# Attention, rational MoE and Sinkhorn MoE in one kernel: a reordered prologue, two weight chunks split inside it, and extra identity matmuls

## The chip, the core and the metric

One core of a Trainium2 chip runs one program. The time is the device time of one execution in microseconds (us); a median of three executions stands for the kernel before. TensorE (PE) does the matmuls, VectorE (DVE), ScalarE (ACT) and GpSimd (POOL) the elementwise work, and SyncE (SP) issues most DMAs. Each engine takes its instructions in the order of its own queue.

## The reference

```
B,H,S,D = 4,8,576,64                     # attention, window 32, plain (heads 0-3) or dilated by 4 (heads 4-7)
attn = softmax(mask(q @ k.T / sqrt(D))) @ v
x    = attn.transpose(0,2,1,3).reshape(2304, 512)
h    = x @ w_in                           # 512 x 2048, float64 in HBM
P    = a0 + a1*h + a2*h^2 + a3*h^3
Q    = 1 + |b0|*|h| + |b1|*h^2
x2   = (P / (Q + 1e-6)) @ w_out           # 2048 x 512
gate = 8 rounds of row and column normalisation of exp(x2 @ w_gate - max)
out  = sum_e gate[:, e] * (relu(x2 @ w1[e]) @ w2[e])     # 8 experts, 512 x 1024 x 512
```

## The kernel before, in words

The program has three stages. A **prologue** computes the attention of batch 0. A **rational loop** of 96 steps (6 token blocks of 384 times 16 slices of 128 hidden columns) computes x2, and the attention of batches 1 to 3 is spread over its steps. Then the expert stage runs to the end.

Batch 0 has 12 groups (head pair `pr`, part `jj`) and its work is cut into pieces: 16 `prep` (transposes of q or k on PE, copied out of PSUM by ACT), 12 `qk` (a mask matmul L363, score matmuls L370; then DVE's maximum L388, ACT's three `Exp` L390, DVE's normalisation L394 and L395, POOL's multiply L396), 12 `tr` (transposes L405, copied out by ACT L410) and 12 `av` (L429; then a 16-bit high part by ACT L229 and a low part by DVE L232, in the scale `s_x1`). `s_x1` comes from a scan of the absolute maximum of half of v (`v_load`, `v_scan` L484) and a chain `pow2_scale` that starts at L207 and passes through PE (L180). `att_load` fetches q and k of one head pair, `att_load_v` the windows of v of one group.

`w_in` comes in four chunks of 512 columns. `wi_load` fetches a chunk as 64-bit words, `wi_conv` turns each of its four 128-row parts into float32 (ACT's `Prelu` L492, DVE's L496 and L497) and takes its absolute maximum (ACT L526), `wi_scale` makes its scale and the coefficients of the rational function, and `wi_split` makes the high and low half-precision parts (ACT L229, DVE L232, 128x512). `wo_load` and `wo_split` do the same for the 16 slices of `w_out`, with L492, L496, L497, L607 and POOL's L611. A loop step takes 12 matmuls L634 to L636 (`h1ps`), the rational function on ACT and DVE that begins at ACT's L657, and five steps later (`LAG`) 12 matmuls L694 to L696.

What runs when is decided in two places. The prologue is a list of pieces with extra calls hung on piece numbers (`extra`), and the loop has numbered slots, four to a step (`at`), filled from tables: `WI_S` for the chunks of `w_in`, `WO` for the slices of `w_out`, and rows of calls for the scan of v's second half. After that a scheduler orders each engine's queue by its own timeline, with attention pieces at raised priority. `load` ties a DMA to the last matmul recorded in `gate_mm`, so that it isn't issued earlier. PSUM has eight one-bank tiles in two rotating groups of four.

Of the kernel before, what the change touches and what calls it, by code (L numbers as in the profile page):

```python
# [10 lines left out]
F32 = mybir.dt.float32  # L11
# [16 lines left out]
def kernel(  # L28
# [14 lines left out]
    nc = tc.nc  # L43
# [287 lines left out]
    def att_prep(b, pr, x):  # L331
# [27 lines left out]
    def att_qk(b, pr, jj):  # L359
# [6 lines left out]
        for i in range(3):  # L366
            j = 3 * jj + i
            for h in range(2):
                hd = slice(h * D, (h + 1) * D)
                nc.tensor.matmul(  # L370
                    bt[hd, i * KW:(i + 1) * KW],
                    st["qT"][hd, j * 64:(j + 1) * 64],
                    st["kT"][hd, j * 64:j * 64 + KW],
                    start=False,
                    stop=i == 2,
                )
        sc = bt[:, 0:3 * KW].rearrange("q (i c) -> q i c", i=3)
        i = b * NG + pr * 3 + jj
# [8 lines left out]
        def after():  # L387
            nc.vector.tensor_reduce(out=sx[:, 0, :], in_=sc, axis=AX, op=ALU.max, negate=True)  # L388
            for i in range(3):
                nc.scalar.activation(p[:, i, :], sc[:, i, :], AF.Exp, bias=sx[:, 0, i:i + 1], accum_out=sx[:, 1, i:i + 1])  # L390
            return norm
# [30 lines left out]
    def att_av(b, pr, jj):  # L422
# [4 lines left out]
        for h in range(2):  # L427
            for i in range(3):
# [51 lines left out]
    def v_scan(hf, i):  # L480
        t = vst.pop((hf, i))
        m = vmx[:, 6 * hf + 2 * i:6 * hf + 2 * i + 2]
        for j in range(2):
            nc.vector.tensor_reduce(out=m[:, j:j + 1], in_=t[:, j * NV // 2:(j + 1) * NV // 2], axis=AX, op=ALU.max, apply_absolute_value=True)  # L484
# [4 lines left out]
    def to_f32(src, y, dst):  # L489
        w = src.rearrange("p (n two) -> p n two", two=2)  # L490
        lo, hi = w[:, :, 0], w[:, :, 1]
        nc.scalar.activation(y, hi.bitcast(F32), AF.Prelu, scale=float(2.0**-112), alpha=-float(2.0**32))  # L492
        d = y.bitcast(I32)
# [27 lines left out]
    def wi_conv(c, kk):  # L521
# [10 lines left out]
        junk = st[:, 0:512].bitcast(F32)  # L532
        bits = to_f32(st, x, x)

# [55 lines left out]
    def wo_split(f):  # L590
# [23 lines left out]


    behind = {}

    def pin(eng, i):
        if eng in behind:
            tc.add_manual_dep(i.ins, behind[eng], mybir.DependencyInfo(mybir.DependencyClass.Sync, mybir.DependencyReason.DATA), reason="behind work that others wait for")  # L620

# [3 lines left out]
    def rat_l1(st, half):  # L625
# [6 lines left out]
        for kk in (2 * half, 2 * half + 1):  # L632
# [505 lines left out]
    ATT = ((1, 0, 14), (2, 15, 38), (3, 43, 62))  # L1138
    WO = [f if f < 8 else 11.75 + (f - 8) // 2 * 1.5 + 0.5 * (f % 2) for f in range(NF1)]
    WI_S = (None, 0, 4, 7.5)  # L1140

# [48 lines left out]
    def at(s, fn, *a):  # L1190
        slots[s].append((fn, a))
# [95 lines left out]

    for c in range(1, 4):
        s = int(4 * WI_S[c])
        for kk in range(KD):  # L1290
            at(s + 1 + 2 * kk, wi_conv, c, kk)
            at(s + (12 if c > 1 else 11) + kk, wi_split, c, kk)
        at(s + 10, wi_scale, c)
    for c in (2, 3):
        at(int(4 * WI_S[c]) - (6 if c == 2 else 4), wi_load, c)
    at(4 * 20, lambda: load(wgr, w_gate.rearrange("(k p) e -> p k e", p=P)))
    at(4 * 26 + 1, wg_prep)
    for i in range(3):
# [27 lines left out]
    for kk in range(KD):  # L1326
# [95 lines left out]
```

## Time and profile before

| | us |
|---|---|
| median of 3 executions | 1957.07 (1953.51 to 1958.82) |
| the profiled execution | 1955.98 |
| its span, first to last instruction | 1954.0 |
| mean granted TensorE clock | 0.981 of full speed |
| PE busy | 1875.1 (96%) |
| DVE busy | 1543.8 (79%) |
| ACT busy | 1217.3 (62%) |
| POOL busy | 493.2 (25%) |

The busy shares are averages over stages with different limits. Of the 40 slices of the span that the page shows, PE is at its lowest in the first four, and the granted clock is below nine tenths in the first three alone. The first 48.9 us slice shows PE, DVE, ACT and the DMA engines at 6, 4, 5 and 6 tenths.

### The profile page before, as it was taken

What the parts mean: (1) busy time and instruction counts of PE and PEld (TensorE: products, weight loads), DVE (VectorE), ACT (ScalarE), POOL (GpSimd) and SP (SyncE); (2) the same over time, 40 slices, a digit from 0 to 9 for tenths busy, and PEclk for the clock granted to TensorE, in tenths of its full rate; (3) what the DMA queues carried; (4) which work ended last, traced back from release to release, by engine and by line L of the source; (5) the groups of instructions that cost most, each with busy time, mean ns of one, the idle gap of its engine ahead of it and who ended that gap; (6) DMA issues with size and microseconds to landing.
All of it is one profiled execution on the core that took longest, in us unless ns stands there. A gap on an engine that the chain in (4) does not pass through costs nothing. (4 is left out here: it accounts for less than half of the span.)

```text
span 1954.0 us, 36520 instructions
## 1 busy us (share of the span) xinstructions
PE 1875.1 (96%) x14202; PEld 1410.8 (72%) x14202; DVE 1543.8 (79%) x2516; ACT 1217.3 (62%) x2182; POOL 493.2 (25%) x489
## 2 busy tenths in 40 slices
PE   6688999999999899999999999999999999999998
PEld 5466777777776677777777777777777777777776
DVE  4799769678998999778688778877878787786754
ACT  5788777777776545647556655664656566465652
POOL 1233422222232023015113211411421231141110
PEclk6789999999999999999999999999999999999999
DMA  6744113122212351564454357345435534633323
GB/s 172 214 135 125 32 38 104 34 59 76 92 38 80 124 157 68 190 185 128 94 141 125 56 120 184 69 109 143 103 62 135 155 74 112 165 87 78 86 54 53
DMA packets 208269, 207.92 MB, mean 106 GB/s; under 512 B 78176, under 2 KB 155488, under 8 KB 208096
## 3 DMA queue, kind: packets, MB, share of 16 engines
q1 hardware_dynamic: 191232, 173.09, 29.4%
q0 software_dynamic: 16864, 32.51, 11.2%
q8 instruction: 111, 1.82, 0.4%
q14 instruction: 62, 0.51, 0.1%
HBM read 155.86 MB, written 49.68 MB: 105 GB/s over the span
## 5 line engine op out<-in xcount | busy, mean ns | idle before, releaser
L922 PEld LDWEIGHTS <-roomA 128*128 128x128 f16 x3276 | 318.9, 98 | 182.1 <-issue 14.2
L922 PE MATMUL l1a<-roomA 128*128 128x384 f16 x1872 | 355.8, 326 | 3.3 <-ACT roomV L971 2.5
L922 PE MATMUL l1b<-roomA 128*128 128x384 f16 x1404 | 273.6, 326 | 5.4 <-DVE roomA L973 3.4
L680 POOL TENSOR_TENSOR roomIG<-roomA,roomIG 128x384 fp32r<-128x384 f32 x96 | 118.2, 1242 | 230.6 <-ACT roomIG L679 206.0
L944 POOL TENSOR_TENSOR roomIG<-roomA 128x384 f32<-128x384 f32 x48 | 60.2, 1254 | 456.8 <-ACT roomA L978 344.3
L1022 PE MATMUL yps<-roomA 128*128 128x256 f16 x630 | 169.9, 273 | 2.4 <-DVE roomV L1048 1.5
L1022 PE MATMUL yps<-roomA,roomV 128*128 128x256 f16 x630 | 168.9, 273 | 3.1 <-DVE roomA L1045 3.1
L1023 PE MATMUL yps<-roomA,roomV 128*128 128x256 f16 x630 | 170.5, 273 | 0.8 <-DVE roomA L885 0.8
L1023 PE MATMUL yps<-roomA 128*128 128x256 f16 x630 | 170.9, 273 | 0.0
L1024 PE MATMUL yps<-roomA,roomV 128*128 128x256 f16 x630 | 169.4, 273 | 0.0
L1024 PE MATMUL yps<-roomA 128*128 128x256 f16 x630 | 169.1, 273 | 0.0
L871 POOL TENSOR_TENSOR roomA<-roomA 128x256 f32<-128x256 f32 x140 | 133.2, 971 | 35.0 <-DVE roomA L885 23.1
L695 PE MATMUL o1ps<-roomIG,roomV 128*128 128x384 f32 x384 | 137.0, 357 | 1.5 <-POOL roomIG L680 1.2
L885 DVE SCALAR_TENSOR_TENSOR roomA<-roomA,sm 128x768 f16<-128x768 f32 (+1 forms) x92 | 112.2, 1232 | 25.1 <-ACT roomA L882 24.3
L634 PE MATMUL h1ps<-roomA 128*128 128x384 f16 x384 | 128.5, 335 | 2.7 <-DVE roomA L660 1.3
L696 PE MATMUL o1ps<-roomIG,roomV 128*128 128x384 f32 x384 | 130.0, 341 | 0.0
L636 PE MATMUL h1ps<-roomA 128*128 128x384 f16 x384 | 127.9, 333 | 0.2 <-DVE roomA L232 0.2
L635 PE MATMUL h1ps<-roomA 128*128 128x384 f16 x384 | 128.0, 333 | 0.0
L944 POOL TENSOR_TENSOR roomIG<-roomV 128x384 f32<-128x384 f32 x48 | 51.1, 1064 | 288.7 <-ACT roomV L978 246.7
L1022 PEld LDWEIGHTS <-roomA 128*128 128x128 f16 x1008 | 98.4, 98 | 28.7 <-DVE roomA L1048 3.4
L1023 PEld LDWEIGHTS <-roomV 128*128 128x128 f16 x1008 | 98.4, 98 | 27.4 <-issue 4.2
L882 ACT ACTIVATE roomA<-roomA,sm 128x768 f16<-128x768 f32 (+1 forms) x92 | 93.9, 1036 | 38.9 <-POOL roomA L871 17.0
(221 smaller groups left out, 4925.5 us busy)
## 6 DMA issues: line engine op xcount, KB each, us to landing
roomA<-xd SPq DMA_DIRECT2D x119, 384.0 KB
roomA<-in_moe_w_dram SPq DMA_DIRECT2D x240, 128.0 KB
roomA<-in_moe_w_dram SPq DMA_DIRECT2D x120, 256.0 KB
out_dram<-roomV POOLq DMA_DIRECT2D x31, 512.0 KB, 5.7
out_dram<-roomA POOLq DMA_DIRECT2D x31, 512.0 KB, 5.8
roomV<-in_moe_w_in_dram SPq DMA_DIRECT2D x16, 512.0 KB
roomA<-in_moe_w_out_dram SPq DMA_DIRECT2D x16, 512.0 KB
xd<-roomA SPq DMA_DIRECT2D x14, 384.0 KB
```

The costliest lines, as they stand in the source:

```text
L634: mm = nc.tensor.matmul(hp, whi, xb[:, 0, kk, :], start=kk == 0, stop=False)
L635: nc.tensor.matmul(hp, whi, xb[:, 1, kk, :], start=False, stop=False)
L636: nc.tensor.matmul(hp, wlo, xb[:, 0, kk, :], start=False, stop=kk == KD - 1)
L680: nc.gpsimd.tensor_tensor(out=gl, in0=g, in1=gh.bitcast(F32), op=ALU.subtract)
L695: nc.tensor.matmul(ob[dd], hi, d["gl"], start=False, stop=False)
L696: nc.tensor.matmul(ob[dd], lo, d["gh"], start=False, stop=last)
L871: pin("p" if pool else "v", eng.tensor_tensor(out=d[:, o, :], in0=a, in1=b, op=ALU.add if w == 0 and n == 0 else ALU.subtract))
L885: pin("v", nc.vector.scalar_tensor_tensor(out=l, in0=x, scalar=sc, in1=h, op0=ALU.mult, op1=ALU.subtract))
L922: mm = nc.tensor.matmul(ps, w[:, wx_, wh, kk * P:(kk + 1) * P], x[:, xh, kk, :], start=start and kk == 0 and wh == 0 and xh == 0, stop=sto ...
L1022: nc.tensor.matmul(o, hh[:, a - 1, c], w[:, m, 0, :], start=i == 0 and half == 0, stop=False)
L1023: nc.tensor.matmul(o, hh[:, a - 1, c], w[:, m, 1, :], start=False, stop=False)
L1024: nc.tensor.matmul(o, hl[:, a - 1, c], w[:, m, 0, :], start=False, stop=i == NP - 1 and (last or half == 1 or b == 3))
```

## The change

1. SP's queue is given q and k of head pair 2 ahead of v's scan, the coefficients `ra` and `rb` after v's first windows, then chunk 0 of `w_in`, then pair 3. Chunk 1 of `w_in` is requested at piece 20 in place of piece 30.
2. Chunks 0 and 1 of `w_in` are converted, scaled and split at fixed pieces (26 and 36 onward). Before, chunk 0 was split in the last pieces, and the calls for chunk 1 stood in steps 0 to 3 of the loop.
3. After each `prep`, `qk` and `av` piece of batch 0, four matmuls of the identity, read as 16-bit words, write 224 otherwise unused columns of the same PSUM tile (`keep_busy`).
4. `pin` orders an instruction behind a recorded one: the `Prelu` of chunks 0 and 1 behind the last `Exp` recorded, that of chunks 2 and 3 and of `w_out`, and the scan of v's second half, behind a step's first `h1ps` matmul.
5. In the loop, chunks 2 and 3 move to steps 2 and 6 (from 4 and 7.5), the second scan from step 1 to step 6, and slices 8 to 15 of `w_out` are spread evenly.

```diff
+    ident_w = ident.bitcast(BF16)
+    def keep_busy(bt, b, c, count):
+        if b < 1:
+            for _ in range(count):
+                nc.tensor.matmul(bt[:, c:c + 224], ident_w[:, 0:P], ident_w[:, 0:224], start=True, stop=True)
...
         for c in range(n):
             nc.tensor.transpose(bt[:, c * w:(c + 1) * w], src[:, n * y + c, :], ident[:w, :w])
+        keep_busy(bt, b, HS, 4)
...
+        keep_busy(bt, b, 3 * KW, 4)
         sc = bt[:, 0:3 * KW].rearrange("q (i c) -> q i c", i=3)
...
-                nc.scalar.activation(p[:, i, :], sc[:, i, :], AF.Exp, bias=sx[:, 0, i:i + 1], accum_out=sx[:, 1, i:i + 1])
+                e = nc.scalar.activation(p[:, i, :], sc[:, i, :], AF.Exp, bias=sx[:, 0, i:i + 1], accum_out=sx[:, 1, i:i + 1])
+            behind["x"] = e.ins.name
...
+        keep_busy(bt, b, 288, 4)
...
+            if hf:
+                pin("m", r)
...
-        nc.scalar.activation(y, hi.bitcast(F32), AF.Prelu, scale=float(2.0**-112), alpha=-float(2.0**32))
+        i = nc.scalar.activation(y, hi.bitcast(F32), AF.Prelu, scale=float(2.0**-112), alpha=-float(2.0**32))
+        pin(late, i)
...
-        bits = to_f32(st, x, x)
+        bits = to_f32(st, x, x, "x" if c < 2 else "m")
...
-            bits = to_f32(x, y, y)
+            bits = to_f32(x, y, y, "m")
...
                 gate_mm[0] = mm.ins
+                behind["m"] = mm.ins.name
...
-    WO = [f if f < 8 else 11.75 + (f - 8) // 2 * 1.5 + 0.5 * (f % 2) for f in range(NF1)]
-    WI_S = (None, 0, 4, 7.5)
+    WO = [f if f < 8 else f + 2.25 for f in range(NF1)]
+    WI_S = (None, None, 2, 6)
...
-    at(4 * 13, coefs, 1, 0, 4)
+        at(4 * 6 + 8 * i, v_load, 1, i, "x2_4")
+        at(4 * (6 + 2) + 8 * i, v_scan, 1, i)
+    at(4 * 13, v_scale, 1)
+    at(4 * 14 + 2, coefs, 1, 0, 4)
...
     att_load(0, 1, "R1")
+    att_load(0, 2, "R2")
+    for i in range(3):
+        v_load(0, i, f"x2_{3 + i}")
+    for i in range(2, 4):
+        att_load_v(i)
     nc.sync.dma_start(out=abt[:, 0:4], in_=ra.partition_broadcast(P))
     nc.sync.dma_start(out=abt[:, 4:6], in_=rb.partition_broadcast(P))
-    for i in range(3):
-        v_load(0, i, f"x2_{3 + i}")
-    att_load(0, 2, "R2")
-    for i in range(2, 4):
-        att_load_v(i)
+    wi_load(0)
+    att_load(0, 3, "R3")
     for i in range(4, 8):
         att_load_v(i)
-    att_load(0, 3, "R3")
...
-    extra[12].append(lambda: wi_load(0))
-    extra[30].append(lambda: wi_load(1))
+    extra[20].append(lambda: wi_load(1))
...
-        extra[30 + 2 * kk].append(lambda kk=kk: wi_conv(0, kk))
-        extra[n - 4 + kk].append(lambda kk=kk: wi_split(0, kk))
-    extra[n - 4 - 1].append(lambda: wi_scale(0))
+    for c, x in ((0, 26), (1, 36)):
+        for kk in range(KD):
+            extra[x + kk].append(lambda c=c, kk=kk: wi_conv(c, kk))
+            extra[x + 8 + kk].append(lambda c=c, kk=kk: wi_split(c, kk))
+        extra[x + 7].append(lambda c=c: wi_scale(c))
```

On SP, from the second head pair's q and k onward, the queue of the kernel before holds these rows (`in_v_dram` with 128x1536 is v's scan, `abt` the coefficients; L166 is `load`):

```order
L280 DMA roomA<-in_q_dram 96x6x64 x2
L280 DMA roomA<-in_k_dram 96x6x64 x2
L1309 DMA abt<-in_moe_a_dram 128x4
L1310 DMA abt<-in_moe_b_dram 128x2
L166 DMA roomA<-in_v_dram 128x1536 x3
L280 DMA roomA<-in_q_dram 72x8x64 x2
L280 DMA roomA<-in_k_dram 72x8x64 x2
L304 DMA roomA<-in_v_dram 96x3x64 x2
```

From the same point the changed kernel's queue holds these:

```order
L293 DMA roomA<-in_q_dram 96x6x64 x2
L293 DMA roomA<-in_k_dram 96x6x64 x2
L293 DMA roomA<-in_q_dram 72x8x64 x2
L293 DMA roomA<-in_k_dram 72x8x64 x2
L166 DMA roomA<-in_v_dram 128x1536 x3
L317 DMA roomA<-in_v_dram 96x3x64 x2
L315 DMA roomA<-in_v_dram 64x2x64
L317 DMA roomA<-in_v_dram 96x2x64 x2
L1328 DMA abt<-in_moe_a_dram 128x4
L1329 DMA abt<-in_moe_b_dram 128x2
L166 DMA roomV_136<-in_moe_w_in_dram 128x1024 x2
L166 DMA roomV_139<-in_moe_w_in_dram 128x1024 x2
```

Between v's scan and chunk 0 of `w_in` there are now five loads of v's windows and the two of the coefficients; before there were four for pair 2, 17 for v and four for pair 3. Pair 3's four and 17 for v come next, and then chunk 1; before, 18 for v stood between chunk 0 and chunk 1.

On ACT, around the first `Prelu` of chunk 0 (L492; `p` and `roomA,sx` are exponentials, `avps` parts of x), the kernel before has:

```order
L390 ACTIVATE p,sx<-scps,sx 128x96 x6
L229 ACTIVATE roomA<-avps,sm 128x192
L492 ACTIVATE roomV_268<-roomV_268 128x512
L390 ACTIVATE roomA,sx<-scps,sx 128x96 x3
L229 ACTIVATE roomA<-avps,sm 128x192
L492 ACTIVATE roomV_268<-roomV_268 128x512
```

The changed kernel has, around its first `Prelu` of chunk 0 (L511) and up to that of chunk 1 (which reads `roomV_255`):

```order
L405 ACTIVATE roomA,sx<-scps,sx 128x96
L511 ACTIVATE roomV_136<-roomV_136 128x512 x2
L405 ACTIVATE roomA,sx<-scps,sx 128x96 x2
L235 ACTIVATE roomA<-avps,sm 128x192
L369 ACTIVATE roomV_255<-qkps 128x288 x2
L511 ACTIVATE roomV_136<-roomV_139 128x512 x2
L369 ACTIVATE roomV_255<-qkps 128x288
L546 ACTIVATE roomV_136,sm<-roomV_136 128x512
...
L405 ACTIVATE roomA,sx<-scps,sx 128x96 x3
L235 ACTIVATE roomA<-avps,sm 128x192
L511 ACTIVATE roomV_139<-roomV_255 128x512 x2
```

The conversions stay among the exponentials and copies of batch 0, with the `Prelu`s in pairs.

On PE, the first score matmuls of head pair 1 (`scps<-roomV`) stood in one run in the kernel before:

```order
L405 MATMUL ptps<-ident,p 96x128 x3
L363 LDWEIGHTS ident_b
L363 MATMUL scps<-masks,ident_b 128x288
L370 MATMUL scps<-roomV_221 64x96 x18
L429 MATMUL avps<-roomA 64x64 x6
```

In the changed kernel each six of the eighteen are followed by four pairs of weight load and matmul on the identity (the first pair is shown, and then the next av):

```order
L421 MATMUL ptps<-ident,p 96x128 x3
L377 LDWEIGHTS ident_b
L377 MATMUL scps<-masks,ident_b 128x288
L384 MATMUL scps<-roomV_255 64x96 x6
L254 LDWEIGHTS ident
L254 MATMUL scps<-ident 128x224
...
L445 MATMUL avps<-roomA 64x64 x6
```

The program adds 160 such pairs, four for each of the 40 pieces.

## Rows read from the trace of the kernel before

**Rows 1.** Busy time by stretch: five engines, PE clock, DMA share, GB/s.
```profile
0.00:26.00 26.00, 17.19 (x139) 14.13 (x139) 12.54 (x43) 12.71 (x52) 6.44 (x24) 0.80 0.67 184
26.00:71.00 45.00, 27.76 (x258) 21.12 (x257) 24.32 (x71) 29.50 (x101) 4.76 (x9) 0.61 0.61 174
76.00:140.00 64.00, 52.70 (x392) 37.13 (x390) 61.27 (x123) 55.90 (x150) 23.44 (x22) 0.92 0.61 188
140.00:200.00 60.00, 52.68 (x399) 38.85 (x399) 55.06 (x115) 48.84 (x125) 22.44 (x21) 0.91 0.40 110
200.00:300.00 100.00, 100.00 (x763) 78.76 (x762) 72.58 (x132) 75.06 (x189) 33.18 (x37) 1.00 0.16 41
```

**Rows 2.** ACT's waits from 0 to 76 us: total, times, longest.
```profile
ACT roomV L492 <- DMA roomV<-in_moe_w_in_dram: 11.9, 2, 7.3
ACT roomA L390 <- DVE sx L388: 6.5, 4, 3.4
ACT roomA L355 <- PE qkps L347: 5.2, 3, 3.1
```

**Rows 3.** Timeline of ACT: start, duration, instruction, idle before and its cause.
```profile
25.22 0.41 ACT L229 ACTIVATE roomA<-avps,sm 128x192 f16<-128x192 f32 x1
40.64 0.66 ACT L492 ACTIVATE roomV<-roomV 128x512 f32<-128x512 f32 x1 [7.27 <-DMA roomV<-in_moe_w_in_dram]
54.90 0.66 ACT L492 ACTIVATE roomV<-roomV 128x512 f32<-128x512 f32 x1 [4.63 <-DMA roomV<-in_moe_w_in_dram]
75.18 0.67 ACT L657 ACTIVATE roomA<-h1ps,cf 128x384 f32<-128x384 f32 x1
215.58 0.67 ACT L657 ACTIVATE roomA<-h1ps,cf 128x384 f32<-128x384 f32 x1 [0.35 <-PE h1ps L636]
```

**Rows 4.** Timeline of SP's queue in the prologue.
```profile
34.39 3.13 SPq L166 DMA_DIRECT2D roomV<-in_moe_w_in_dram  x4
37.63 12.99 SPq L315 DMA_DIRECT2D roomA<-in_v_dram  x18
50.69 1.85 SPq L166 DMA_DIRECT2D roomV<-in_moe_w_in_dram  x4
```

**Rows 5.** ACT by line and form, 0 to 220 us: busy us, mean ns.
```profile
L229 ACT ACTIVATE roomA<-roomV,sm 128x512 f16<-128x512 f32 x16 | 10.3, 728 | 1.4 <-DVE sm L225 1.4
L355 ACT ACTIVATE roomA<-qkps 128x288 f32<-128x288 f32 x32 | 13.3, 431 | 5.4 <-PE qkps L347 5.2
```

**Rows 6.** Busy time by stretch, two shorter ones.
```profile
14.00:16.00 2.00, 0.00 (x0) 0.09 (x1) 0.89 (x6) 1.08 (x7) 0.67 (x1) 0.85 1.00 418
20.00:30.00 10.00, 8.96 (x65) 7.04 (x65) 5.31 (x20) 6.80 (x27) 2.15 (x4) 0.50 0.49 105
```

**Rows 7.** Timeline of PE, third pair's transposes, av matmuls, first loop step.
```profile
36.83 1.19 PE L347 MATMUL qkps<-ident,roomA 72*128 72x72 f32 x8 [2.36 <-issue]
...
26.92 1.18 PE L429 MATMUL avps<-roomA 96*64 96x64 f32 x12
...
33.28 0.73 PE L429 MATMUL avps<-roomA 96*64 96x64 f32 x12
...
72.60 0.53 PE L634 MATMUL h1ps<-roomA 128*128 128x384 f16 x1
72.92 0.53 PE L635 MATMUL h1ps<-roomA 128*128 128x384 f16 x1
...
73.50 0.33 PE L634 MATMUL h1ps<-roomA 128*128 128x384 f16 x1
73.66 0.33 PE L635 MATMUL h1ps<-roomA 128*128 128x384 f16 x1
```

**Rows 8.** Timeline of DVE, the wait for the coefficients.
```profile
14.24 0.21 DVE L559 TENSOR_SCALAR sm<-abt 128x1 int32<-128x1 int32 x2 [2.22 <-DMA abt<-in_moe_b_dram]
```

**Rows 9.** ACT's waits from 76 to 218 us.
```profile
ACT roomA L657 <- PE h1ps L636: 3.7, 4, 2.2
```

More of the change, by code (lines that the diff above doesn't have):

```diff
@@ L198, in across_sum, with pin @@
         nc.vector.tensor_scalar(out=out_, in0=bt[:, 0:n], scalar1=1e-9, scalar2=None, op0=ALU.add)
+    behind = {}
+    def pin(eng, i):
+        if eng in behind:
+            tc.add_manual_dep(i.ins, behind[eng], mybir.DependencyInfo(mybir.DependencyClass.Sync, mybir.DependencyReason.DATA), reason="behind work that others wait for")
     def delayed(fn, k):
@@ L483, in v_scan, with to_f32 @@
         for j in range(2):
-            nc.vector.tensor_reduce(out=m[:, j:j + 1], in_=t[:, j * NV // 2:(j + 1) * NV // 2], axis=AX, op=ALU.max, apply_absolute_value=True)
+            r = nc.vector.tensor_reduce(out=m[:, j:j + 1], in_=t[:, j * NV // 2:(j + 1) * NV // 2], axis=AX, op=ALU.max, apply_absolute_value=True)
+            if hf:
+                pin("m", r)
     def v_scale(hf):
         return pow2_scale(vmx[:, 6 * hf:6 * hf + 6], 6, 14, s_x1[:, hf:hf + 1], i_x1[:, hf:hf + 1], lag=hf)
-    def to_f32(src, y, dst):
+    def to_f32(src, y, dst, late):
         w = src.rearrange("p (n two) -> p n two", two=2)
         lo, hi = w[:, :, 0], w[:, :, 1]
-        nc.scalar.activation(y, hi.bitcast(F32), AF.Prelu, scale=float(2.0**-112), alpha=-float(2.0**32))
+        i = nc.scalar.activation(y, hi.bitcast(F32), AF.Prelu, scale=float(2.0**-112), alpha=-float(2.0**32))
+        pin(late, i)
         d = y.bitcast(I32)
@@ L613, in wo_split @@
         return s1
[L616 to L620, printed above, removed]
     cur = {}
@@ L1286, in run_slot @@
                 at(s + 1, more)
-    for c in range(1, 4):
-        s = int(4 * WI_S[c])
+    for c in (2, 3):
+        s = 4 * WI_S[c]
+        at(s - 6, wi_load, c)
         for kk in range(KD):
             at(s + 1 + 2 * kk, wi_conv, c, kk)
-            at(s + (12 if c > 1 else 11) + kk, wi_split, c, kk)
+            at(s + 12 + kk, wi_split, c, kk)
         at(s + 10, wi_scale, c)
-    for c in (2, 3):
-        at(int(4 * WI_S[c]) - (6 if c == 2 else 4), wi_load, c)
     at(4 * 20, lambda: load(wgr, w_gate.rearrange("(k p) e -> p k e", p=P)))
@@ L1298 @@
     for i in range(3):
-        at(4 * 1 + 8 * i, v_load, 1, i, "x2_4")
-        at(4 * (1 + 2) + 8 * i, v_scan, 1, i)
-    at(4 * (1 + 8), v_scale, 1)
-    at(4 * 13, coefs, 1, 0, 4)
+        at(4 * 6 + 8 * i, v_load, 1, i, "x2_4")
+        at(4 * (6 + 2) + 8 * i, v_scan, 1, i)
+    at(4 * 13, v_scale, 1)
+    at(4 * 14 + 2, coefs, 1, 0, 4)
     att_load(0, 0)
@@ L1325 @@
     n = len(pcs)
-    for kk in range(KD):
-        extra[30 + 2 * kk].append(lambda kk=kk: wi_conv(0, kk))
-        extra[n - 4 + kk].append(lambda kk=kk: wi_split(0, kk))
-    extra[n - 4 - 1].append(lambda: wi_scale(0))
+    for c, x in ((0, 26), (1, 36)):
[3 more added lines that the diff above has]
+        extra[x + 7].append(lambda c=c: wi_scale(c))
     for f in range(2):
```

## Prediction

> **What bounds the kernel now.** I read the busy times by stretch first. From 200 us on PE is busy 100.00 of 100 us at the full clock (2.4 GHz, granted 1.00), so there the time is PE's and nothing that the change moves shortens it [rows 1]. Before that PE isn't the limit. From 76 to 200 us DVE is busy 116.3 of 124 us (61.27 + 55.06) and ACT 104.7, while PE has 18.6 us of idle time: the loop's first steps carry all the conversions and splits of w_in and w_out and wait for DVE and ACT. From 0 to 71 us, the prologue, no engine is the limit by its sum: PE 45.0, DVE 36.9, ACT 42.2 us busy. That is a chain with holes, and PE's clock is 0.80 and 0.61 there, which is much time at 1.2 GHz.
>
> The holes are seen in ACT's waits. The largest is 11.9 us in two waits: the `Prelu` of a chunk of w_in stands in ACT's queue ahead of batch 0's exponentials and waits for its DMA [rows 2], 7.27 us at 40.64 and 4.63 us at 54.90 [rows 3]. ACT is in order, so attention waits behind it. SP's timeline says why: chunk 0 was issued at 34.39, and chunk 1 at 50.69 after 18 small loads that took 12.99 us to issue [rows 4]. The loop's first evacuation (L657) starts at 75.18, that of step 20, where PE has become the limit, at 215.58 [rows 3]. What the change takes from the first, with the work ahead of step 20 unchanged, it takes from the end.
>
> **The waits for w_in.** In the new order chunk 0 follows v's scan and seven small loads. Up to its end SP has asked for 12 loads of 144 KB (pairs 0 to 2), 2.36 MB of scan, about 0.6 MB of v and 2.1 MB of w_in: 6.8 MB. The old queue moved 4.8 MB in 26 us (184 GB/s [rows 1]), and large loads alone ran at 418 GB/s [rows 6]; the remaining 2.0 MB take 5 us, so chunk 0 is there by some 31 us, and ACT, which starts on x at 25.22 [rows 3], comes to its `Prelu` after some 5 us of copies and exponentials, near 31. That wait goes. Chunk 1 then stands behind pair 3 and 17 loads of v. At 12.99/18 = 0.72 us each [rows 4], 21 loads are 15 us; from an issue of chunk 0 that ends near 23 to 25 us it is issued at 38 to 40 and its first part lands 4.2 us later (50.69 to 54.90), at 42 to 44. ACT has by then done about 17 us of work since 25.22 and arrives at 42 to 43. I leave 1 us of wait, with ends of 0 and 5. Term: -11.9 + 1 = -10.9 us.
>
> **v's scale.** The scans now queue behind pair 2, but no longer behind the coefficients. The coefficients queue behind the scans, and on DVE their use stands ahead of the maximum that starts the scale chain. Before, DVE waited 2.22 us for them early on [rows 8]. If they come late now, `s_x1` is late and ACT's first split at 25.22 with it; everything of pairs 0 to 3 that has to leave PSUM is queued behind. Between 2 us better and 4 us worse; I take +1.
>
> **The identity matmuls.** 40 pieces (16 prep, 12 qk, 12 av) times 4 make 160 weight loads and matmuls of 224 columns. The nearest rows are the loop's matmuls of 384 columns with one weight load each: 0.32 us apart at the half clock (72.60 to 72.92) and 0.16 at the full one (73.50 to 73.66) [rows 7]. That bounds the 160 at 26 us (full) or 51 us (half); by columns it would be 15 or 30. PE has 26 us idle in the first 71 [rows 1], so at the full clock they fit; they also lengthen a piece by 0.4 to 0.6 us before its copy, since the built program makes each copy wait for the four matmuls too (the first copy waits for a count of seven: three transposes and four of these). Against that stands the clock: twelve av matmuls take 1.18 us at the half clock and 0.73 at the full one [rows 7], so of some 29 us that PE works at the half clock (27.76 x 0.78 + 17.19 x 0.40, the shares of time that a mean of 0.61 and of 0.80 means [rows 1]) a third could go, 11 us, about half of it where others wait for PE (5.2 us of ACT's waits are for transposes, part of that the first data [rows 2]). Between -6 and +25 us; I take +1, near a draw, because the pieces are pipelined and PE isn't the sum's limit.
>
> Whether they lift the clock at all is open. From 20 to 30 us PE was busy 8.96 of 10 us and the clock stayed at 0.50; at 73 us it rose after PE had begun the loop's matmuls [rows 6, 7]. The Trainium skill (TensorE: Matmul & The Clock Gate, Part 1: The HAM clock gate) says that the throttled clock is the default and that activity releases it; by that rule the 160 pay for themselves and the term is -6. By the row at 20 us, where a nearly full queue released nothing, it is above +1. The skill (PSUM — Partial Sum Buffer, PSUM bank collisions raise a hardware error) also says that no engine may read a bank in which PE writes, whatever the columns, so putting them in a piece's own bank must delay its copy; no run here shows a collision, and the program's counts agree. By that alone the term is 40 times 0.4 to 0.6 us, 16 to 24 us, if nothing overlapped.
>
> **Work moved ahead.** Chunk 1's split adds 4 x 0.73 us on ACT [rows 5] ahead of the first L657 and as much on DVE; a few other small instructions also change sides (a copy is 0.43 [rows 5]). About +3.7 us before the first L657 and -3.7 after it on engines that are full in both places: 0 at the end.
>
> **Pins and the new table in the loop.** 24 `Prelu`s (8 of chunks 2 and 3, 16 of w_out) and the second scan now wait for a step's first matmul. Behind a waiting `Prelu` stand the rational function's and the attention's ACT work, and PE waits for both. Before, ACT waited for PE's h1 four times in 21 steps, 3.7 us [rows 9]. At 0.93 us each, 24 waits would cost 22 us; none, if PE is already past. I take +0.5: in this stretch ACT and DVE are behind PE. The evened table could fill DVE's 7.7 us of idle time between 76 and 200 at most; I count 0, since the instructions ahead of step 20 are the same.
>
> **Sum.** -10.9 + 1 + 1 + 0.5 = -8.4 us. The profiled execution took 1955.98 us, so 1947.6; it lies 1.1 us below the median of the three runs (1957.07), which the result will be set beside: 1948.7 us.
>
> **Rivals.**
> - *The next wait takes the place of the one removed.* Pair 3's transposes waited 2.36 us at 36.83 [rows 7]; if chunk 1, pair 3 or the scale comes 5 us later than I work out, or ACT simply waits at its exponentials (6.5 us for DVE's maxima already [rows 2]), the first L657 stays within 3 us of 75. Then 1955. For it: SP still has to issue all the small loads, 0.72 us each.
> - *The identity matmuls make PE the bound (slower).* If the clock stays at the half level, PE's 45 us of work and up to 51 more are 96 us in a prologue of 71: 25 us on, 10 saved, 15 lost; by columns, 30, PE comes to 75 and the savings are lost in waits. Between 1957 and 1973; I put it at 1968. It decides from the point where the 160 take more than PE's 26 idle us. Against it: at the full clock they take 15 to 26.
> - *More than the waits goes.* The clock stays up, copies come sooner, DVE starts the loop with its backlog done: up to -6 for the clock and -4 in the loop. 1940.
>
> **Chances.** Forecast 0.52 (own range 1944 to 1954), next wait 0.20, PE the bound 0.12, more gained 0.16. This kernel's measurement tells about 0.3% from no change, 5.9 us: faster is below 1951.2, slower above 1962.9. Of the forecast 0.44 is faster and 0.08 the same; more gained is faster, 0.16; of the next wait 0.03 faster, 0.16 the same, 0.01 slower; of PE the bound 0.02 the same, 0.10 slower. Faster 0.63, same 0.26, slower 0.11. The range reaches from the middle of the larger gain to the near end of the slower case: 1938 to 1962.
>
> **What would show it.** ACT's waits should have no L511 for w_in above 2 us in the prologue; the first L672 should start near 67 to 70 us, step 20's near 207; the window from 200 on should look as before. A granted clock near 1.0 from 10 to 60 us would show the identity matmuls at work, one at 0.5 with PE over 90% busy the slower rival. If the first L672 is at 69 and step 20's still at 215, the pins or the table ate the gain. I am wrong if the first L672 is later than 73 us.

## The result and the profile after

After takes 1936.8 us in the median of four runs (1935.4 to 1937.5), before 1957.6 (1953.5 to 1958.8, four runs): ratio 0.9896, 95% interval 0.9879 to 0.9914. The profiled spans are 1935.4 and 1954.0 us. Faster, as forecast, but by 20.8 us where I had 8.4, and 1.2 us below my range.

In after every line past the helpers moves down: the `Prelu` of w_in and w_out is L511 (was L492), a split on ACT L235 (L229), the loop's first evacuation L672 (L657). The identity matmuls are L254. Busy time by stretch, after, against [rows 1]: PE, PEld, DVE, ACT, POOL, then PE's clock, DMA share, GB/s.

```profile
0.00:26.00 26.00, 19.24 (x197) 14.87 (x197) 10.38 (x26) 11.53 (x49) 4.49 (x21) 1.00 0.71 190
26.00:71.00 45.00, 38.24 (x375) 29.36 (x375) 28.72 (x97) 33.63 (x107) 7.68 (x12) 0.81 0.71 212
76.00:140.00 64.00, 52.24 (x393) 37.48 (x392) 56.13 (x118) 56.34 (x152) 25.68 (x23) 0.92 0.52 154
140.00:200.00 60.00, 54.98 (x430) 41.51 (x427) 57.50 (x121) 52.38 (x134) 30.85 (x27) 1.00 0.42 111
200.00:300.00 100.00, 99.26 (x777) 77.14 (x775) 72.58 (x132) 74.64 (x188) 26.30 (x31) 1.00 0.19 50
```

The prologue's clock rose from 0.80 and 0.61 to 1.00 and 0.81, and PE has 12.5 us more work there. ACT's waits from 0 to 76 us, after, against [rows 2]: total, times, longest.

```profile
ACT roomA L369 <- PE qkps L254: 7.0, 6, 4.1
ACT p L405 <- DVE sx L403: 5.4, 4, 1.7
ACT roomA L426 <- PE ptps L421: 5.3, 5, 3.8
ACT roomA L405 <- DVE sx L403: 4.5, 2, 3.3
...
ACT roomV L511 <- DMA roomV<-in_moe_w_in_dram: 0.3, 1, 0.3
```

The 11.9 us for w_in are 0.3. In their place stand copies that wait for identity matmuls (L369 for L254, 7.0 us) and for transposes. ACT's timeline, after, against [rows 3]:

```profile
31.82 0.72 ACT L235 ACTIVATE roomA<-avps,sm 128x192 f16<-128x192 f32 x2
...
48.67 0.66 ACT L511 ACTIVATE roomV<-roomV 128x512 f32<-128x512 f32 x1 [0.32 <-DMA roomV<-in_moe_w_in_dram]
...
76.09 0.67 ACT L672 ACTIVATE roomA<-h1ps,cf 128x384 f32<-128x384 f32 x1
...
203.48 0.67 ACT L672 ACTIVATE roomA<-h1ps,cf 128x384 f32<-128x384 f32 x1 [1.37 <-PE h1ps L650]
```

The first evacuation is 0.9 us later than before, not 6 to 8 earlier; step 20's is 12.1 earlier. The first split of x is at 31.82 instead of 25.22. SP's queue in after, against [rows 4], has v's scan behind head pair 2 (11.35):

```profile
11.35 1.50 SPq L166 DMA_DIRECT2D roomA<-in_v_dram  x3
...
18.44 1.88 SPq L1328 DMA_DIRECT2D abt<-in_moe_a_dram  x1
22.03 0.35 SPq L1329 DMA_DIRECT2D abt<-in_moe_b_dram  x1
23.92 1.75 SPq L166 DMA_DIRECT2D roomV<-in_moe_w_in_dram  x4
...
43.13 1.89 SPq L166 DMA_DIRECT2D roomV<-in_moe_w_in_dram  x4
```

Chunk 0 is issued 10.5 us and chunk 1 7.6 us sooner. DVE's scan (L501), after, is late, and so is the maximum that starts the scale chain: 26.54, in before 22.75. The next maximum (L194) then waits 2.87 us for a PE transpose, in before 0.54; that transpose stands behind av and identity matmuls in PE's queue:

```profile
24.26 1.80 DVE L501 TENSOR_REDUCE sm<-roomA 128x1 f32<-128x768 f32 x2
...
26.54 0.15 DVE L213 TENSOR_REDUCE sm<-sm 128x1 f32<-128x6 f32 x1
...
29.64 0.29 DVE L194 TENSOR_REDUCE sm<-mxps 128x1 f32<-128x128 f32 x1 [2.87 <-PE mxps L180]
```

So the chain that I had read was shortened, another took its place in the prologue, and the time came from somewhere else. By the starts of L657 and L672 the lead of after is -0.9 us at step 0, 10.0 at step 4, 12.1 at step 20, 9.9 at step 50 and 18.6 at the end. I had said that nothing is gained where PE is the limit; in this profile nearly half of the gain arose there, in two later ones of after (e12, e16) 4.3 and 6.5 us of it.

### The profile page after: what moved, and what is told of

Same layout as the page of the kernel before. It is cut to its first block, busy times and chain, and to the rows that moved or that the text cites. A ratio compares the mean times of both kernels' runs of the same rounds, so it can differ in the third digit from the quotient of the medians.

```text
span 1935.4 us, 36839 instructions
## 1 busy us (share of the span) xinstructions
PE 1878.3 (97%) x14362; PEld 1414.8 (73%) x14362; DVE 1535.7 (79%) x2516; ACT 1216.4 (63%) x2182; POOL 497.6 (26%) x489
## 3 DMA queue, kind: packets, MB, share of 16 engines
q0 software_dynamic: 16864, 32.51, 11.4%
## 5 line engine op out<-in xcount | busy, mean ns | idle before, releaser
L937 PEld LDWEIGHTS <-roomA 128*128 128x128 f16 x3276 | 319.6, 98 | 179.7 <-issue 11.4
L886 POOL TENSOR_TENSOR roomA<-roomA 128x256 f32<-128x256 f32 x140 | 131.0, 955 | 35.6 <-DVE roomA L900 18.6
L1038 PEld LDWEIGHTS <-roomV 128*128 128x128 f16 x1008 | 98.7, 98 | 23.7 <-issue 0.7
L1037 PEld LDWEIGHTS <-roomV 128*128 128x128 f16 x1008 | 98.8, 98 | 23.0 <-DVE roomV L1062 0.4
```

The costliest lines, as they stand in the source:

```text
L886: pin("p" if pool else "v", eng.tensor_tensor(out=d[:, o, :], in0=a, in1=b, op=ALU.add if w == 0 and n == 0 else ALU.subtract))
L937: mm = nc.tensor.matmul(ps, w[:, wx_, wh, kk * P:(kk + 1) * P], x[:, xh, kk, :], start=start and kk == 0 and wh == 0 and xh == 0, stop=sto ...
L1037: nc.tensor.matmul(o, hh[:, a - 1, c], w[:, m, 0, :], start=i == 0 and half == 0, stop=False)
L1038: nc.tensor.matmul(o, hh[:, a - 1, c], w[:, m, 1, :], start=False, stop=False)
```

## The experiments

Sixteen runs, each beside runs of before on the same chip. Steps are the starts (us) of the 1st, 5th, 21st and 51st L672 or L657 in one profile (steps 0, 4, 20 and 50); "rest" is the profiled span less the last of these. "Order" is told under e4.

| kernel | median | ratio, 95% | step 0 | 4 | 20 | 50 | rest | order |
|---|---|---|---|---|---|---|---|---|
| before | 1955.5 to 1958.3 | 1 | 75.2 | 108.1 | 215.6 | 379.1 | 1574.9 | B |
| e4 before, one neutral edit | 1949.3 | .9968 (.9954-.9982) | 73.9 | 106.0 | 215.1 | 378.5 | 1568.8 | A |
| e2 before + identity | 1950.7 | .9964 (.9952-.9977) | 72.4 | 103.7 | 213.2 | 377.8 | 1570.2 | A |
| e6 queue alone | 1943.9 | .9947 (.9929-.9964) | 66.5 | 100.0 | 207.8 | 373.4 | 1567.1 | A |
| e9 queue, two chunks inside | 1939.4 | .9907 (.9878-.9935) | 70.6 | 92.4 | 201.9 | 368.4 | 1569.7 | A |
| e10 e9 + pins | 1937.1 | .9893 (.9870-.9915) | 69.4 | 86.0 | 200.2 | 366.4 | 1566.6 | A |
| e7 e10 + new table | 1934.4 | .9901 (.9881-.9921) | 71.1 | 93.8 | 199.4 | 363.3 | 1568.3 | A |
| e15 e7 again | 1934.2 | .9886 (.9866-.9907) | 70.3 | 92.1 | 198.8 | 362.7 | 1568.3 | A |
| after | 1936.8 | .9896 (.9879-.9914) | 76.1 | 98.1 | 203.5 | 369.3 | 1566.1 | A |
| e12 after | 1935.2 | .9884 (.9861-.9907) | 72.5 | 94.0 | 197.8 | 363.6 | 1570.6 | A |
| e16 after | 1935.3 | .9890 (.9872-.9908) | 71.3 | 92.8 | 196.8 | 362.6 | 1568.4 | A |
| e14 after, one neutral edit | 1938.0 | .9905 (.9884-.9926) | 73.4 | 94.8 | 200.4 | 370.0 | 1567.2 | A |
| e1 after - identity | 1943.9 | .9935 (.9916-.9954) | 69.3 | 92.7 | 199.2 | 362.6 | 1577.2 | B |
| e3 after - new table | 1942.1 | .9930 (.9906-.9953) | 72.8 | 89.9 | 200.0 | 364.6 | 1573.2 | B |
| e5 after - pins | 1955.3 | 1.0002 (.9990-1.0015) | 78.5 | 97.7 | 214.9 | 379.0 | 1573.5 | B |
| e13 e5, one neutral edit | 1953.5 | .9980 (.9967-.9992) | 77.4 | 96.3 | 213.6 | 383.2 | 1569.1 | A |
| e8 e1, scan first | 1937.0 | .9910 (.9893-.9928) | 74.8 | 95.3 | 201.9 | 364.8 | 1568.9 | A |
| e11 e3 - identity, scan first | 1947.8 | .9952 (.9933-.9970) | 75.2 | 93.4 | 207.1 | 371.3 | 1574.7 | B |

**The parts alone (e1 to e3).** e1, against after:

```
-        if b < 1:
+        if b < 0:
             for _ in range(count):
```

> The changed kernel without its 160 identity matmuls. Theory A (the gain up to step 50, 9.9 us in the profiled runs, comes from w_in's waits and the split of chunk 1; the identity matmuls are near a draw, as I forecast at +1): 1934 to 1940 us, step 50 within 3 us of the changed kernel's. Theory B (the clock is what pays: it is 0.81 to 1.00 in the prologue now, 0.61 to 0.80 before): 1942 to 1948, step 50 some 5 to 8 us later, and a prologue clock back near 0.6. In both the expert stage may shift by some us with the scheduler's order.

e2 adds `ident_w`, `keep_busy` and its three calls to before, and nothing else.

> The kernel before with the 160 identity matmuls and nothing else. Theory A: 1955 to 1961 us, the waits of 11.9 us for w_in stay and the start of the loop is where it was. Theory B: 1945 to 1951 us, step 50 earlier by 5 to 8 us. The slower rival of the prediction (PE becomes the bound): 1960 to 1970.

e3, against after, sets the loop's slots back to the old ones:

```
-    WO = [f if f < 8 else f + 2.25 for f in range(NF1)]
-    WI_S = (None, None, 2, 6)
+    WO = [f if f < 8 else 11.75 + (f - 8) // 2 * 1.5 + 0.5 * (f % 2) for f in range(NF1)]
+    WI_S = (None, None, 4, 7.5)
-        at(4 * 6 + 8 * i, v_load, 1, i, "x2_4")
+        at(4 * 1 + 8 * i, v_load, 1, i, "x2_4")
...
```

> The changed kernel with the loop's old table: chunks 2 and 3 at steps 4 and 7.5, v's second scan from step 1, w_out's slices 8 to 15 as before. Theory A (the loop's table is worth nothing, as forecast): 1935 to 1940 us and step 20 within 3 us of the changed kernel's. Theory C (the table carries the gain, since the first evacuation of the loop came no earlier, at 76.1 us, and the lead appeared at steps 3 to 11): 1942 to 1950, step 20 later by 6 us or more.

These didn't add up. All three totals lie in the range of the rival theory (B, B and C), but the marks in the front don't: no step 50 or 20 moved as those theories had it. e1 and e3 were 5 to 7 us slower than after although their front, to step 50, was not behind after's: they lost it all in the rest, 1577.2 and 1573.2 us against 1566.1, and neither edit touches anything there.

**The order of the rest (e4).** So I tried an edit that should do nothing:

```
-    at(4 * 20, lambda: load(wgr, w_gate.rearrange("(k p) e -> p k e", p=P)))
+    at(4 * 22, lambda: load(wgr, w_gate.rearrange("(k p) e -> p k e", p=P)))
```

> The kernel before with one load moved that nothing waits for (w_gate asked for at step 22 in place of 20), a control for the scheduler. If the order of the expert stage is a matter of chance, the times after step 50 move by 3 to 9 us either way while step 50 stays within 1 us: 1950 to 1966. If the expert stage's 8.7 us gain belongs to the change, this kernel is within 3 us of the kernel before all along: 1955 to 1960.

It gains 6.7 us (ratio below 1 by its whole interval; the total is 0.7 below my range), 6.1 of them in the rest. The lists of instructions say why. Of TensorE's 13,591 matmuls in before, read back from the last, e1 and e3 share 10,581 with it; after, e2 and e4 share only 7,614 with before, and over 11,000 with each other. The scheduler falls into one of two orders (B is before's, A is after's). The first place on TensorE where e4 leaves before is in the loop, long before the stretch that pays:

```
 L405 MATMUL ptps<-ident,p 96x128 x3
-L694 MATMUL o1ps<-roomIG,roomV_747 128x384 x4
 L363 LDWEIGHTS ident_b
 L363 MATMUL scps<-masks,ident_b 128x288
 L370 MATMUL scps<-roomA 64x96 x6
+L694 MATMUL o1ps<-roomIG,roomV_747 128x384 x4
```

PE's timeline shows the two orders as two lists of stops. Before, in the expert stage, some 66 and 76 us past step 95 (start, duration, instruction, idle before it and its cause):

```profile
650.78 2.11 PE L922 MATMUL l1b<-roomA 128*128 128x384 f16 x12 [1.92 <-DVE roomA L973]
...
661.25 0.27 PE L1022 MATMUL yps<-roomA,roomV 128*128 128x256 f16 x1 [2.07 <-DVE roomA L1045]
```

e4, the same work:

```profile
647.93 1.14 PE L922 MATMUL l1b<-roomA 128*128 128x384 f16 x6 [1.06 <-DVE roomA L973]
...
656.68 0.49 PE L922 MATMUL l1a<-roomA 128*128 128x384 f16 x2 [0.34 <-ACT roomV L971]
```

1.9 us on l1b becomes 1.1, and the 2.1 us stop is gone. e1, though it has all of the change but the 160 matmuls, has before's stop on l1b at the same distance from step 95, to 0.1 us (its stop on yps is 0.4):

```profile
636.07 3.06 PE L937 MATMUL l1b<-roomA 128*128 128x384 f16 x12 [1.91 <-DVE roomA L988]
```

**The order put to the test (e5 to e8, e13, e14).** e5 leaves out all of the change's pins ("x" on the conversions of chunks 0 and 1; "m" on those of chunks 2 and 3 and of w_out, and on the second scan):

```
-        if eng in behind:
+        if eng in behind and eng not in 'xm':
```

> After, with the prologue's two pins ('x' and 'm', the waits that the change hangs on the conversions and scans) left out. TensorE's matmuls of this kernel, read back from the last one, agree with before's for 10,581 of them and with after's for only 7,614. Theory A (the gain past step 50 is the order that the scheduler happened to choose for the rest): the span after step 50 is before's kind, 1573 to 1577 us, as in the two other kernels with before's order there, and the whole 5 to 10 us over after, whatever the front does; step 50 within 4 us of after's 369.3. Theory B (the rest is shorter because the front arrives earlier and leaves less to catch up): the rest stays at 1566 to 1568 as in after, and the whole within 3 us of after's 1936.8.

e6, before with the new queue alone (the SyncE lines of the diff, and):

```
-    extra[12].append(lambda: wi_load(0))
-    extra[30].append(lambda: wi_load(1))
+    extra[20].append(lambda: wi_load(1))
```

> Before with nothing of the change but SyncE's order in the prologue and chunk 1's load ahead of piece 20. Its matmuls agree with after's for the last 12,160 and with before's for 7,614. Theory A: the rest after step 50 is after's kind, 1566 to 1570. For the front: if the wait for w_in is what the front's gain is, the waits of 3.9 and 8.0 us go to under 2 together and step 50 comes at 368 to 373 (before 379.1), the whole at 1937 to 1944. Theory C (the front's gain comes from converting and splitting two chunks inside the prologue, not from the queue): step 50 stays within 3 us of 379, the whole at 1945 to 1950.

e7 is e1 with the edit of e4:

> After without the 160 identity matmuls (e1) and with the w_gate load asked for at step 22 instead of 20, an edit that by itself does nothing in the front but turns the order of the rest from before's kind to after's kind (the last 11,557 matmuls agree with after's, 7,614 with before's). Theory A: step 50 where e1 has it, 361 to 364, the rest 1566 to 1570 instead of e1's 1577, the whole 1932 to 1938, 6 to 11 us under e1's 1943.9 and at or under after's. Theory D (the identity matmuls themselves shorten the rest, as the one that left them out lost it): the rest stays at 1574 to 1578 and the whole at 1941 to 1946.

e8 is e1 with the scan's loads ahead of pair 2:

```
-    att_load(0, 2, "R2")
     for i in range(3):
         v_load(0, i, f"x2_{3 + i}")
+    att_load(0, 2, "R2")
```

> After without the identity matmuls and with v's three scan loads asked for ahead of pair 2 of q and k, as before the change. Order of the rest of after's kind (the last 11,557 matmuls). If v's scale, now set by a scan that lands late, holds the front: the first split of x moves from e1's 27.5 to 23 to 26, and step 50 to 358 to 361. If pair 2, now later, holds it as much: step 50 stays at 361 to 365. Rest 1566 to 1570 by theory A, so a whole of 1929 to 1936.

The rests came out as said: 1573.5 for e5, 1567.1, 1568.3 and 1568.9 for e6 to e8. The totals of e6 and e7 lie in their ranges, e8's is 1.0 over; e6's waits for w_in are 8.6 us together where I had said under 2. e1 and e7 are the cleanest pair: fronts alike to 0.7 us (362.6 and 363.3 at step 50), wholes 1943.9 and 1934.4.

But "rest" isn't the same work in all kernels. Its mark is an instruction of ACT, and in e1, e3, e5 and e11 12 matmuls stand behind it on TensorE that in the others stand ahead of it; that makes some 2 us of these four rests. A stretch of the same matmuls is found by counting TensorE's records back from the end: from the 11,400th, some 30 us behind step 50, to the 7,624th, where the two orders have become one. It holds the same matmuls in every kernel (in e2 and e10 all but seven). First e1, then e7 (columns as above; a window also counts what reaches into it at its edges):

```profile
398.34:931.62 533.28, 517.87 (x3781) 387.37 (x3778) 468.61 (x739) 343.09 (x546) 136.35 (x117) 0.99 0.38 112
```

```profile
396.98:924.20 527.22, 515.86 (x3781) 385.56 (x3778) 468.01 (x739) 343.36 (x547) 136.25 (x118) 1.00 0.39 113
```

The same work takes 6.1 us less, 4.1 of them in PE's idle time (15.4 against 11.4). Over all profiles this stretch takes 531.9 to 533.7 us in the five with order B and 526.2 to 529.2 in the thirteen with order A, on average 5.2 us less. The clock doesn't explain it: e3 and e11 have order B at 1.00 throughout, and take 531.9 and 532.3. Behind it, where both orders are the same, the time to the end is 1004.4 to 1008.2 us with B and 1005.3 to 1008.0 with A. So the time differs where the order differs, and only there.

e8's first split came at 23.6 as expected, but step 0 was later (74.8) and nothing was won: pair 2, now later, holds as much (PE waits 9.6 us for q's loads there, 4.5 in e7).

Theory A fell in part on the totals, though. e5 was not 5 to 10 us over after but 18.5, with step 50 at 379.0. e13 (e5 with `wg_prep` asked for at slot 106 instead of 105) has order A:

> e5 (after without the two prologue pins) with the preparation of w_gate's tile asked for one slot later, 106 instead of 105: nothing but the order of the rest should change, from before's kind to after's (last 11,557 matmuls as after's). Theory A: step 50 within 4 us of e5's 379.0, the rest after it 1566 to 1571 instead of 1573.5, the whole 1945 to 1950 against e5's 1955.3. What is then left to after's 1936 (9 to 14 us) is the pins' with the new table. Rival H (the pins' loss in e5 was the order alone): the whole at 1936 to 1940. If the order has no effect: 1953 to 1957.

Its rest is 1569.1 as said, and the stretch of the same matmuls is 4.4 us shorter (533.3 to 528.9). But the whole went down by 1.8 us alone (4.3 by the ratios); it missed the 1945 to 1950 and lies in the 1953 to 1957 of "no effect". Ahead of that stretch e13 lost 2.1 us against e5 and behind it 2.2, which is within what three profiles of after differ by there (6.7 and 2.4). For the pins, e14 is the kernel to compare with, the same edit in after, where it leaves order A:

> After with the same edit, 106 instead of 105; here it leaves the order of the rest of after's kind (last 11,634 matmuls). The control: theory A has the whole within 3 us of after (1933 to 1939), the rest after step 50 1566 to 1571. A whole of 1941 or more would say that any edit of the order costs, or this slot in particular.

1938.0, rest 1567.2: the edit by itself is worth nothing that can be measured. e13 differs from it by the missing pins alone, on the same chip: they cost 15.5 us, 13.2 of them by step 50.

**The front, part by part (e9 to e11).** e9 is e3 without pins and identity, so queue and two chunks inside; e10 has the pins too (and slot 106); e11 is e3 without identity and with the scan first.

> The queue's new order (e6) and, beyond it, only the conversions and splits of w_in's first two chunks inside the prologue: the old table of the loop, no pins, no identity matmuls. TensorE's order of the rest agrees with after's (last 12,268 matmuls). Theory F (the part of the change that I put at nothing is the one that pays: VectorE has next to no idle in loop steps 0 to 4, so chunk 1's block of 4 L496, 4 L497 and 4 L232, worked out at 10 us from before, lengthens them, while in the prologue it stands in idle time): the first step a few us later than e6's 66.5, at 68 to 72, but steps 0 to 4 take 17 to 24 us instead of e6's 33.5, and step 50 comes 8 to 13 us ahead of e6's 373.4, at 360 to 366. Rival G (pins or the new table, not the moved chunk, are what e1 has over e6): step 50 within 4 us of 373. Rest by theory A 1566 to 1570; whole 1930 to 1938 by F, 1940 to 1945 by G.

> After without the identity matmuls and with the old table, the pins kept, and the preparation of w_gate's tile asked for one slot later (106 instead of 105), which gives the rest after's order (last 11,034 matmuls). Against e9 it differs by the pins. If the pins are needed only by the new table: step 50 as in e9 within 3 us; if they pay by themselves: 5 to 10 us earlier. If the identity matmuls cost the same 5 to 7 us here as they do with the new table, step 50 is at 357 to 361 (e3, with them, 364.6), the rest 1566 to 1570, the whole 1926 to 1932: under both before and after.

> As e10 with v's scan loads ahead of pair 2 in SyncE's queue (and w_gate's tile at its old slot); rest of after's order (last 11,557). e8 against e1 and e7 showed a first split 4 us earlier and step 50 1.5 to 2 us later. The same here: first split at 23 to 25, step 50 within 3 us of e10's, whole within 4 us of it.

e9 lies between theory F and rival G: step 50 came 5.0 us ahead of e6's, neither 8 to 13 nor within 4, and its total of 1939.4 is 1.4 us over F's range and 0.6 under G's. Steps 0 to 4 take 21.8 us (e6 33.5, before 32.9), as F had it, but not for F's reason. The stretch from step 0 to step 4, first before, then e9:

```profile
75.18:108.05 32.87, 26.51 (x199) 18.43 (x198) 30.02 (x63) 28.40 (x78) 10.05 (x9) 0.90 0.74 218
```

```profile
70.58:92.39 21.81, 15.12 (x115) 9.01 (x113) 19.87 (x41) 21.42 (x61) 6.14 (x7) 0.84 0.82 279
```

DVE is busy 30.0 of before's 32.9 us: the loop starts against DVE. But e9's stretch holds less work, not the same work faster. 24 of TensorE's `o1ps` matmuls (6.2 us) stand ahead of step 4's mark in before, and in e6, and behind it in e9; e9's lead over e6 is 7.6 us at step 4, 1.0 at step 8 and 5.9 at step 20. And the block that F meant is mostly not chunk 1's. DVE by line in before, same stretch:

```profile
L497 DVE SCALAR_TENSOR_TENSOR roomV<-roomV 128x512 int32<-128x512 int32 x4 | 3.5, 868 | 0.0
L232 DVE SCALAR_TENSOR_TENSOR roomA<-roomV,sm,roomA 128x512 f16<-128x512 f32 x4 | 2.8, 739 | 0.0
...
L496 DVE TENSOR_SCALAR roomV<-roomV 128x512 int32<-128x512 int32 x4 | 1.6, 416 | 0.0
```

These are 7.9 us (the 10 in my expectation counted w_out's L496 for w_in's), but L496 and L497 here are chunk 2's. The calls for chunk 1 stood in the loop, yet the scheduler had already put its four conversions into before's prologue: ACT's `Prelu`s from 54.90 [rows 3] to 60.35, DVE's part from 55.60 to 62.2. e9 has chunk 2's in steps 0 to 4 as well:

```profile
L517 DVE SCALAR_TENSOR_TENSOR roomV<-roomV 128x512 int32<-128x512 int32 x4 | 2.7, 682 | 0.0
L516 DVE TENSOR_SCALAR roomV<-roomV 128x512 int32<-128x512 int32 x4 | 2.7, 676 | 0.0
```

What the change moves out of the loop is chunk 1's scale and its four splits (L232, 2.8 us on DVE), into a prologue where DVE is busy 24 to 32 of 45 us. Step 0 comes 4.1 us later for it than in e6 (70.6 against 66.5), and from there to step 50 e9 takes 9.1 us less (297.8 against 306.9), with 4.5 us less work on DVE and, since more of batch 0 is done by step 0, 6.0 less on PE. Which of these makes the 5.0 us, no run separates.

e10's gain over e9 is within the intervals; step 50 at 366.4 missed the 357 to 361, and the whole of 1937.1 the 1926 to 1932. e11 has the other order, against its expectation (it shares its last 10,581 matmuls with before; the 11,557 that the expectation says aren't this kernel's), and a front 5 us behind e10's. So its whole of 1947.8 missed too, as did its first split (26.3); the scan stays behind pair 2.

What the pins do is seen on ACT. e5, ACT's timeline, chunk 2's `Prelu`s (other rows left out) and the first L672:

```profile
62.26 0.66 ACT L511 ACTIVATE roomV<-roomV 128x512 f32<-128x512 f32 x1
64.01 0.66 ACT L511 ACTIVATE roomV<-roomV 128x512 f32<-128x512 f32 x1
69.71 0.66 ACT L511 ACTIVATE roomV<-roomV 128x512 f32<-128x512 f32 x1
73.32 0.73 ACT L511 ACTIVATE roomV<-roomV 128x512 f32<-128x512 f32 x1
...
78.52 0.65 ACT L672 ACTIVATE roomA<-h1ps,cf 128x384 f32<-128x384 f32 x1
```

After, chunk 2's four stand behind it:

```profile
76.09 0.67 ACT L672 ACTIVATE roomA<-h1ps,cf 128x384 f32<-128x384 f32 x1
...
82.66 1.22 ACT L511 ACTIVATE roomV<-roomV 128x512 f32<-128x512 f32 x2
83.77 0.67 ACT L672 ACTIVATE roomA<-h1ps,cf 128x384 f32<-128x384 f32 x1
...
89.34 1.26 ACT L511 ACTIVATE roomV<-roomV 128x512 f32<-128x512 f32 x2
```

The pin keeps the scheduler from pulling later work ahead. (With the old table it doesn't pull this far without pins either: e9 has chunk 2's four behind its third L672.) With the old table the pins also end most of the wait for w_in, which I had put down to the queue. ACT's waits from 0 to 76 us, first e9 (no pins), then e10 (with pins):

```profile
ACT roomV L511 <- DMA roomV<-in_moe_w_in_dram: 8.7, 3, 5.9
```

```profile
ACT roomV L511 <- DMA roomV<-in_moe_w_in_dram: 1.3, 2, 0.8
```

These 7.4 us brought step 50 forward by 2.0. With the new table the wait is small without pins, too (e5 2.0, e13 3.7 us; with them 0.3 to 3.8 in after, e12, e16 and e14), so the 15.5 us aren't this wait.

**The identity matmuls (e12, e15, e16).** e12 and e16 are after again, e15 is e7 again.

> After itself, on the same chip and beside the same runs of before as e9 to e11, for the comparison with them, and a second profile of one kernel: by theory A the marks of the order come back (step 50 at 369 within 1.5 us, rest 1565 to 1569), the median 1935 to 1939.

> e7 again (after without the identity matmuls, order of the rest of after's kind), five rounds beside after itself. If the identity matmuls cost 4 to 7 us, as the first profiles say at step 50: 1930 to 1933 against 1936. If they cost next to nothing in the whole, as the medians so far say (1934.4 against 1936.8 and 1935.2): within 2.5 us of e16.

> After itself, five rounds, for e13 to e15 to be read against: 1934 to 1938 by all theories. Its step 50, 369.3 and 363.6 in two profiles so far, shows in a third how far one profile's mark of the front can be trusted: 362 to 371.

Three profiles of after have step 50 at 369.3, 363.6 and 362.6, so the 6.7 us that e1 seemed to save there belonged to one profile; e12 missed its 369, and its rest of 1570.6 the 1565 to 1569. With and without the 160, on one chip: 1935.3 and 1934.2, ratios 0.9890 and 0.9886. PE by line and tile, after:

```profile
L254 PE MATMUL qkps<-ident 128*128 128x224 bf16 x64 | 11.0, 301 | 0.0
...
L254 PE MATMUL avps<-ident 128*128 128x224 bf16 x48 | 7.4, 282 | 0.0
L254 PE MATMUL scps<-ident 128*128 128x224 bf16 x48 | 7.1, 273 | 0.0
```

25.5 us of PE's time (23.6 in e16) go with a rise of the prologue's clock from 0.90 and 0.64 (e15) to 1.00 and 0.92 (e16). PE's busy time from 0 to 71 us grows by 6.8 us alone, from 51.0 to 57.8: the rest of the 160's time is given back by the other matmuls. The whole doesn't change by what can be measured, and no run beats after by more than that.

## Why the prediction was wrong

**Two steps failed.** The first is "from 200 us on PE is busy 100.00 of 100 us ..., so there the time is PE's and nothing that the change moves shortens it". A window of 100 us stood for 1750. That window did look as before in after (99.26 of 100 us), and still the stretch of the same matmuls behind step 50 is on average 5.2 us shorter with order A than with order B, whatever the front (eighteen profiles, before and after included, and the two groups don't overlap); an edit that does nothing else gains 6.7. The order of the two kernels differs there, and I took it for neutral without a row for it. The second is "Work moved ahead", a term put at 0 that is worth 4.5 to 7.8 us (e9 against e6).

By ratio against before, along the kernels with order A and times 1957 us, the gain is: order 6.3 us, queue 4.1, two chunks inside 7.8, pins 2.7, new table 0, identity 0; 20.9 together, 20.4 measured. By the plain medians it is 6.7, 5.4, 4.5, 2.3, 2.9 and -1.1. The intervals of the ratios leave some 3 us of uncertainty on the first step, 4 on the queue and 5 to 7 on the others, so that of the single steps only the order and, just, the two chunks stand clear of it. The order is held up by the stretch of the same matmuls, too.

- *Waits for w_in, -10.9.* They went, to 0.3 us (2.4 and 1.6 in the other two profiles), but not as I put it: the queue alone leaves 8.6, of them 5.8 for chunk 1, where I had 1 with ends of 0 and 5; in after chunk 1 is issued at 43.13, where I had 38 to 40. The moved calls alone leave 8.7 (e9), and the pins end most of that (e10). And the wait on ACT wasn't the price: e10, without it, has step 50 just 2.0 us earlier, and e8 waits 6.8 us for w_in and is 2.6 us behind e7. Step 0 didn't come at 67 to 70 but at 71.3 to 76.1. "I am wrong if the first L672 is later than 73 us": it was, in the first profile, and the total was better than I said.
- *Work moved ahead, 0.* The block was the right one, chunk 1's split; "engines that are full in both places" was the mistake: in the prologue DVE wasn't full [rows 1]. That queue and moved chunk together, 9.9 us by the medians and 11.9 by the ratios, are near the 9.9 that I had summed for the waits and the scale is luck: they come by another path.
- *v's scale, +1.* Its sign holds in after, 25.2 to 31.8 for the first split (28 in the other two profiles), and half of its mechanism: the scan is late behind pair 2, but the coefficients that I feared kept nobody waiting, and the 2.87 us for the PE transpose I hadn't seen. e8 got the split back and won nothing, so its price at the end is nothing that shows.
- *Identity matmuls, +1.* Right in size: near a draw. They fit PE's idle time (25.5 us, my bound at the full clock was 26), the clock rose and the copies waited. The Trainium skill (TensorE: Matmul & The Clock Gate, Part 1: The HAM clock gate) says that activity releases the clock; the trace agrees, 1.00 where it was 0.80 [rows 1]. The -6 that I took from it didn't come: the released PE spends what it wins, and 6.8 us more, on the 160.
- *Pins and table, +0.5.* Sign wrong. A pin is a place in the order and not only a wait: with the old table the pins are worth some 2 to 3 us, within the noise (e9, e10), with the new one 15.5 (e13 against e14).

**The rivals.** "More than the waits goes", 1940, came nearest, yet of its reasons (clock, backlog of DVE) the clock gave nothing, and DVE's part is what e9 leaves open. "The next wait takes the place" is true of step 0 and false of the end. PE never became the bound (38.24 of 45 us busy in after).

**What stays open.** Why the scheduler has just these two orders; whether DVE's or PE's smaller load behind step 0 carries the gain of e9; and where without the pins steps 10 to 20 lose 8 us (e13 65.7 us, after 57.5): single waits of up to 3.3 us on all engines, none that explains it. Order B on after itself was not run; the pairs before and e4, e1 and e7, e5 and e13 stand for it.

## What to carry to other kernels

Where a scheduler places the instructions, run a neutral edit first: if the time moves by what you hope to gain, compare orders to the last instruction and compare only kernels of one order. Compare stretches that hold the same instructions: a mark on one engine can cut another engine's queue at different places, as steps 4 and 50 did here. Before a moved block is priced, look where the scheduler had put it, and at the idle time of its engines at both places; the wait that it had caused wasn't its price here. One profile's mark in the front is good to some 7 us here; medians on one chip, and a second profile, decide what is smaller.

## What the runs showed that I had not expected

- Three executions of the same program (after) reach step 50 at 369.3, 363.6 and 362.6 us and differ by 4.4 us in the whole (spans 1935.4, 1934.2, 1931.0). The late one had v's last scan start at 24.26 us, the others at 22.76 and 22.16, and a granted clock of 0.81 from 26 to 71 us against 0.89 and 0.92.
- The slowest kernels spread most: before 1951 to 1963 us over all its runs, e13 1948 to 1956, after 1933 to 1938.
- With the 160 matmuls of 224 columns the granted clock is 1.00 through the first 26 us (0.97 in e5), without them 0.80 to 0.90. Even alone on before (e2, 1.00 and then 0.81) they change the whole by nothing that can be told from e4's order (.9964 and .9968).
